# Second weight matrix of the first channel group converted inside the mixers' first run, with both stated orders written anew

## The chip, the cores and the metric

The kernel runs on one core of a Trainium2 chip. The metric is device time in microseconds (us). Three runs of the kernel before took 602.53, 602.62 and 603.88 us, so its median is 602.62 us. A further execution was profiled: it took 602.69 us, and its trace spans 600.90 us from the first instruction to the last. The other 1.79 us lie around the span.

## The reference

Attention with rotary positions for 4 batches of 8 heads (576 positions, 64 values a head), then a token mixer and a channel mixer, each two matrix products with a ReLU between them and a residual sum. Everything is float32 at the outside; the four weight matrices arrive as 64-bit floats.

```python
q_rot, k_rot = rotate(q), rotate(k)                       # 4 x 8 x 576 x 64
scores = q_rot @ k_rot.T / sqrt(64)
attn = softmax(scores)                                     # exp(scores - max) / (sum + 1e-9)
x = (attn @ v).transpose(0, 2, 1, 3).reshape(4, 576, 512)

h = relu(x.transpose(0, 2, 1) @ w_tok1) @ w_tok2           # 576 -> 256 -> 576
u = x + h.transpose(0, 2, 1)
out = u + relu(u @ w_ch1) @ w_ch2                          # 512 -> 1536 -> 512
```

## The kernel before, in words

Attention works on 16 pairs of heads. For each, the rotated q and k are transposed on TensorE, scores come in blocks (line L593), VectorE takes the row maxima (L493) and ScalarE the exponentials (L497), TensorE turns the result over (L616), ScalarE or VectorE copies it out of PSUM (L621), and TensorE multiplies with v (L634). VectorE scales by the row sums and writes X (L668; XT, L674, for the tail rows).

The mixers multiply in split form: each float32 operand is kept as a high and a low part, and three matmuls (high·high, low·high, high·low) stand for one product. The token mixer is L819 (first product) and L841 (second); its residual sum into X is L844. The channel mixer cuts the 576 x 4 rows into five chunks and the 1536 columns into four groups. For each chunk `up` transposes u (L910), casts the high part out of PSUM on ScalarE (`uh`, L915) and takes the low part on VectorE (`ul`, L916). `cm1` multiplies with the group's part of w_ch1 (L936: 36 matmuls for a chunk, then gh on ScalarE, L938, and gl on VectorE, L940). `cm2` multiplies with its part of w_ch2 (L963: 9 matmuls for each block of 128 rows, then the sum into X on VectorE, L965).

Weights go through `f64_split`, a chain of ten tasks for each block of 128 rows after its load (L738): ScalarE L709 (into fa) and L711 (into fc), a clamp L713 (VectorE or GpSimd), VectorE L715 (shift), L717 (into fh) and L719, a product L721 and a sum L723 (VectorE or GpSimd), the cast of the high part on ScalarE (L729) and the difference that gives the low part (L730, VectorE or GpSimd). There are two stg, two fa and two fh buffers and one fc. For a group, w_ch1 is four blocks of 128x384 (results c1h, c1l) and w_ch2 three blocks of 128x512 (c2h, c2l). Three blocks of eleven tasks are the 33 tasks of the title.

The order is set by a planner. `plan.run(ORDER1)` places 1666 tasks in a stated order, a number each that also picks the engine: attention, the token weights and the tokens of batch 0. `plan.run(ORDER2)` places 162 more, the mixers' first run: tokens of batches 1 to 3, w_ch1 of group 0, and `up` for chunks 0 and 1. A third call, `plan.run()` without an order, places the rest greedily, by when a task can start and by priority: `up` for chunks 2 to 4, all `cm1` and `cm2`, the weights of groups 1 to 3 and, in the kernel before, w_ch2 of group 0. Each engine then executes its own instructions in the order in which they were placed, and waits on the others by semaphores. PSUM has eight banks for the mixers (`m_...`).

```python
held = weights(0, AT["wg"][0], (1,))            # w_ch1 of group 0
for ci in range(2):
    ups[ci] = up(ci, AT["up"][ci])
plan.run(ORDER2)
...
weights(0, 1000, (2,), held)                     # w_ch2 of group 0
for ci in range(2, NC):
    ups[ci] = up(ci, 1000 + 100 * ci - 120)
```

Of the kernel before, what the change touches and what calls it, by code (L numbers as in the profile page):

```python
# [64 lines left out]

class Task:
# [8 lines left out]
class Plan:  # L75
# [53 lines left out]
    def place(self, t, s, eng, dur, fn):  # L129
# [13 lines left out]
        fn()  # L143
# [3 lines left out]
        self.clock[eng] = end  # L147
# [64 lines left out]
AT = {'load': [1.46, -95.74, 1755.84, -446.16, -10.32, -39.47], 'rot': [-30.33, -28.71, -413.29, -24.98], 'pt': [2461.71, -120.88, 1877.09, 0.03], 'qk': [-19.92, -94.77, -29.81, -42.47, -64.18, 1974.42, -445.69, 27.95, -11.96, -66.6, -413.71, -4.28, -3.14, 1684.05, 2036.62, 1632.15, 1700.12, -3.39, -14.08, 1717.83], 'mx': [-18.32, -97.08, -28.47, -222.21, 6.35, 102.54, -32.49, -15.54, 1579.98, 1593.71, -66.46, 1669.44, -16.89, 1934.18, 1942.38, -85.25, -54.68, -66.81, 1912.69, -8.83, 1697.35, 2415.63, 1609.9, 23.08, -40.85, -271.23, 8.19, -10.94, -20.04, -405.36, -59.72, -406.05, 2099.98, 1.92, 1651.83, 1951.2, 1677.89, 1499.17, -7.34, 1632.2], 'ex': [-19.75, -25.79, -97.92, -19.73, 1983.61, 1573.24, -17.98, -1.23, -9.94, -101.57, 88.51, 1713.87, -29.01, 1630.6, -9.17, 1879.5, 1922.03, -18.78, -23.18, 19.55], 'tr': [-261.73, 1684.38, -347.64, 1853.57, -223.18, 1740.33, -18.09, 1625.16, -353.85, 2050.66, -65.51, 2482.09, -74.23, -25.76, 1924.68, -6.29, -550.16, 2116.11, -49.33, -19.36], 'cp': [-285.8, 1993.92, -15.28, -338.61, -33.12, -32.9, 1494.57, -414.57, -230.35, -354.01, -214.2, -9.85, -35.68, -247.66, -14.87, -307.76, -26.24, 90.92, 1865.89, 2189.31], 'pv': [1983.73, 10.91, -453.58, -23.11], 'p1': [-52.7, -56.83, 1864.91, -1.75], 'fin': [2216.99, -20.0], 'tok': [1652.21, 1875.86, 1482.41, 2166.22, -11.87, 1947.96], 'inv': [-8.92, -3.44], 'f6': [1767.81, 1652.44], 'tk': [1968.59, -7.94, -26.45, -12.06], 'pre': [-2.55], 'tm': [-283.71, 77.1, 1499.3, -17.97, 1601.75, -59.36, 1543.29, -96.53, -111.26, 1974.16, 1626.79, -49.74], 'wg': [1621.69], 'up': [3.65, 1617.77], 'ti': [5.61]}  # L212
ORDER1 = (
# [106 lines left out]
def rope_attention_mixer_kernel(ctx: ExitStack, tc: tile.TileContext, q, k, v, w_tok1, w_tok2, w_ch1, w_ch2, tab, out):  # L320
# [8 lines left out]
    nc = tc.nc  # L329
# [28 lines left out]
    def attention(ctx):  # L358
# [703 lines left out]
```

## Time and profile before

| | us |
|---|---|
| median of three runs | 602.62 |
| profiled execution | 602.69 |
| its span | 600.90 |
| TensorE (PE) busy | 585.6 (97% of the span) |
| VectorE (DVE) busy | 385.3 (64%) |
| ScalarE (ACT) busy | 312.4 (52%) |
| GpSimd (POOL) busy | 309.3 (51%) |

Busy shares are averages over stages with different limits. Attention and the tokens of batch 0 fill the span up to about 251 us, the mixers' first run goes on to about 288 us for the first products and to 295 us for the last second product, and the channel mixer takes the rest. PE counts a matmul as busy up to a modelled end, so a stretch with 100% can still hold matmuls that follow one another a little late. PEld is the weight load that runs ahead of the matmuls.

### The profile page before, as it was taken

Reading aid. Unit: us, or ns where it says so; the run is one execution under the profiler, and the core shown is the slowest. Engines: PE = TensorE matmul, PEld = TensorE weight load, DVE = VectorE, ACT = ScalarE, POOL = GpSimd, SP = SyncE. Lnnn points to the kernel's source line nnn. Section 1 sums busy time; section 2 is a strip of 40 time slices with the busy share of each in tenths; the row PEclk is TensorE's granted clock in tenths of the full one; section 3 lists DMA queues with packets and bytes.
Section 4 is the critical chain, followed back from the end, with each engine's and each line's share of the span. In section 5 each row is a group of like instructions: output and inputs, shape, how many; then the busy total and the mean of one; then the engine's idle time right before and its main releaser. Section 6 shows DMA issues by size and latency. Waiting matters only on the chain.

```text
span 600.9 us, 12684 instructions
## 1 busy us (share of the span) xinstructions
PE 585.6 (97%) x4825; PEld 461.0 (77%) x4825; DVE 385.3 (64%) x1121; ACT 312.4 (52%) x796; POOL 309.3 (51%) x258
## 2 busy tenths in 40 slices
PE   4999999999999999999999999999999999999997
PEld 3777676777677777687777888888888888888886
DVE  6998999998899988688845545445423443223232
ACT  3998999999999988243464332233202311110110
POOL 4997876888868531023578686477503760000000
PEclk9999999999999999999998999999999999999999
DMA  5443242313311201001122222122101200001123
GB/s 151 126 116 86 71 108 75 105 29 90 101 52 60 62 2 31 25 26 62 36 65 76 71 61 54 60 71 55 50 1 36 71 0 1 1 1 70 71 70 106
DMA packets 34093, 36.15 MB, mean 60 GB/s; under 512 B 13808, under 2 KB 27632, under 8 KB 34032
## 3 DMA queue, kind: packets, MB, share of 16 engines
q1 hardware_dynamic: 33200, 35.01, 20.3%
q8 instruction: 38, 0.62, 0.4%
q10 hardware_dynamic: 832, 0.33, 0.2%
q14 instruction: 23, 0.19, 0.1%
HBM read 30.61 MB, written 4.72 MB: 59 GB/s over the span
## 4 chain that ended last, share of the span: by engine, by line
PE 95%; DVE 2%; DMA 1%; ACT 1%; issue 0%; DVEq 0%
PE m L936 25%; PE m L963 24%; PE s L634 14%; PE s L593 11%; PE s L616 7%; PE m L841 3%; PE m L819 3%; PE s L471 2%; PE s L516 2%; PE s L819 1%; PE s L537 1%; PE s L663 1%; PE s L841 1%; DMA tabs<-in_tab_dram 1%; DVE p L493 0%; DMA kraw<-in_k_dram 0%
## 5 line engine op out<-in xcount | busy, mean ns | idle before, releaser
L938 ACT ACTIVATE gh<-m 128x512 fp32r<-128x512 f32 (+1 forms) x60 | 33.3, 555 | 174.0 <-PE m L936 170.8
L497 ACT ACTIVATE p<-p,nm 128x576 f32<-128x576 f32 x128 | 98.9, 778 | 1.7 <-DVE p L493 1.1
L940 DVE SCALAR_TENSOR_TENSOR gl<-m,gh 128x512 fp32r<-128x512 f32 (+1 forms) x60 | 38.1, 637 | 93.3 <-ACT gh L938 93.2
L965 DVE TENSOR_TENSOR X<-m,X 128x512 f32<-128x512 f32 (+1 forms) x65 | 44.4, 683 | 74.0 <-PE m L963 73.9
L936 PE MATMUL m<-uh,c1h 128*128 128x512 f32 (+1 forms) x240 | 89.1, 371 | 0.1
L936 PE MATMUL m<-ul,c1h 128*128 128x512 f32 (+1 forms) x240 | 88.9, 370 | 0.0
L936 PE MATMUL m<-uh,c1l 128*128 128x512 f32 (+1 forms) x240 | 88.9, 370 | 0.0
L634 PE MATMUL s<-pt,vraw 128*64 128x256 f32 (+1 forms) x640 | 84.7, 411 | 0.0
L963 PE MATMUL m<-c2l,gh 128*128 128x512 f32 (+1 forms) x219 | 84.6, 386 | 0.0
L963 PE MATMUL m<-c2h,gh 128*128 128x512 f32 (+1 forms) x219 | 84.6, 386 | 0.0
L963 PE MATMUL m<-c2h,gl 128*128 128x512 f32 (+1 forms) x219 | 84.6, 386 | 0.0
L593 PE MATMUL s<-kt,qt 64*128 64x288 f32 x512 | 80.9, 430 | 1.2 <-ACT kt L482 0.9
L721 POOL TENSOR_TENSOR fa<-fc,fa 128x512 f32<-128x512 f32 (+2 forms) x30 | 35.9, 1197 | 75.2 <-DVE fa L719 63.4
L634 PEld LDWEIGHTS s<-pt,vraw 128*64 128x64 f32 x640 | 43.1, 137 | 30.1 <-DVE p L493 1.3
L493 DVE TENSOR_SCALAR_CACHE_REDUCE p<-s,nm 128x288 f32<-128x288 f32 x128 | 62.3, 512 | 3.8 <-PE s L593 1.7
L621 ACT COPY pt<-s 128x320 f32<-128x320 f32 (+1 forms) x172 | 60.6, 408 | 4.9 <-PE s L616 3.4
L616 PEld LDWEIGHTS s<-ident,p 64*128 64x128 f32 x1152 | 47.0, 139 | 17.5 <-ACT p L497 8.1
L593 PEld LDWEIGHTS s<-kt,qt 64*128 64x128 f32 x512 | 51.1, 192 | 8.7 <-ACT pt L621 1.7
L493 DVE TENSOR_SCALAR_CACHE_REDUCE p<-s 128x288 f32<-128x288 f32 x128 | 53.9, 452 | 4.4 <-PE s L593 4.0
L713 POOL TENSOR_SCALAR fa<-fa 128x512 f32<-128x512 f32 (+3 forms) x30 | 50.9, 1699 | 9.5 <-ACT fa L709 9.4
L616 PE MATMUL s<-ident,p 64*128 64x64 f32 x1152 | 52.6, 226 | 0.3 <-ACT p L497 0.2
L936 PEld LDWEIGHTS m<-uh,c1h 128*128 128x128 f32 x240 | 45.5, 190 | 8.1 <-DVE ul L916 0.3
(130 smaller groups left out, 1061.8 us busy)
## 6 DMA issues: line engine op xcount, KB each, us to landing
stg<-in_moe_w_ch_dram SPq DMA_DIRECT2D x16, 384.0 KB, 3.2
stg<-in_moe_w_ch_dram SPq DMA_DIRECT2D x12, 512.0 KB, 3.7
vraw<-in_v_dram SPq DMA_DIRECT2D x16, 256.0 KB, 3.2
kraw<-in_k_dram SPq DMA_DIRECT2D x15, 256.0 KB, 3.2
qraw<-in_q_dram SPq DMA_DIRECT2D x15, 256.0 KB, 3.3
out_dram<-X SPq DMA_DIRECT2D x15, 256.0 KB, 2.3
stg<-in_moe_w_tok_dram SPq DMA_DIRECT2D x4, 512.0 KB, 4.3
kraw<-in_k_dram SPq DMA_DIRECT2D x32, 32.0 KB, 2.9
```

Of the source, the lines that this page charges most:

```text
L493: return lambda: nc.vector.tensor_scalar(out=p()[:, c * W2:(c + 1) * W2], in0=sb.t[:, 0:W2], scalar1=-D ** -0.5, scalar2=nm.t[:, 0:1] if c ...
L497: return lambda: nc.scalar.activation(out=p(), in_=p(), func=ACTF.Exp, bias=nm.t[:, 1:2], scale=-1.0, accum_out=l())
L593: nc.tensor.matmul(sbs[h].t[:, 0:W2], flat(qt.t)[halves[h], TL + j * P:TL + (j + 1) * P], flat(kt.t)[halves[h], TL * (1 - h) + u * W2:TL * ...
L616: nc.tensor.transpose(xy[z].t[:, i * TL:(i + 1) * TL], pb.t[halves[z], c0:c0 + P], ident[halves[z], halves[z]])
L621: return lambda: e(out=pt[c].t[:, R * h:R * h + m, o + z * TL:o + (z + 1) * TL], in_=xy[z].t[:, 0:m * TL].rearrange("p (r s) -> p r s", r=m))
L634: nc.tensor.matmul(ab.t[halves[h], 0:w], vb.t[:, h, r, :], m, start=(r == 0), stop=(r == R))
L713: clamp = lambda e: lambda: e.tensor_scalar(out=A(), in0=A(), scalar1=EXP_LO, scalar2=EXP_HI, op0=ALU.max, op1=ALU.min)
L721: mul_ = lambda e: lambda: e.tensor_tensor(out=A(), in0=C(), in1=A(), op=ALU.mult)
L936: nc.tensor.matmul(tb.t[:, 0:n], a, m, start=(i == 0), stop=(i == len(lst) - 1))
L940: y = add("DVE", dve(n), lambda f=f, tb=tb: nc.vector.scalar_tensor_tensor(out=gb.t[1][:, f, 0:n], in0=tb.t[:, 0:n], scalar=0.0, in1=gb.t[ ...
L963: nc.tensor.matmul(tb.t[:, 0:w], a, m, start=(i == 0), stop=(i == len(lst) - 1))
L965: y = add("DVE", dve(w) + 0.08, lambda u=u, tb=tb, cols=cols, w=w: nc.vector.tensor_tensor(out=u[:, cols], in0=tb.t[:, 0:w], in1=u[:, cols ...
```

## The change

The call that makes the 33 conversion tasks of w_ch2, group 0, now stands ahead of `plan.run(ORDER2)`. ORDER2 has 195 entries in place of 162, and all of them are new. ORDER1 has the same 1666 tasks and is written anew as well; 166 of them run on another engine than before (the copies L621 for one: 160 on ScalarE where there were 172). The third, greedy run has the same priorities as before, without these 33 tasks.

The diff also brings code for pairs of PSUM banks that are read by one instruction (`duo`, `Half`, `none`, `mx1`, `cp1`, `f51` and a few more). It acts only on numbers listed in `MERGED`, which is empty. `clock` may no longer go back in the planner, and the buffers of a task are listed once each.

```diff
+MERGED = ()
 ORDER1 = (
-    68, 84, 0, 16, 88, 8, 20, 24, 28, 36, 4, 92, 12, 96, 104, 40, 44, 48, 76, 100, 52, 64, 72, 60, 80, 108, 112, 116, 148, 156, 152, 32, 56, 1408, 1428,
+    68, 0, 84, 16, 20, 88, 24, 92, 96, 100, 28, 12, 4, 8, 40, 32, 44, 104, 48, 52, 64, 60, 56, 72, 80, 76, 36, 1464, 108, 112, 116, 120, 132, 128, 1472,
...
 ORDER2 = (
-    6688, 6692, 7056, 7060, 6680, 6700, 6696, 6684, 7252, 6665, 7064, 6668, 7232, 7256, 6708, 6673, 6676, 6704, 7068, 6716, 7072, 7076, 7080, 6784, 6788,
+    7056, 7064, 6692, 6688, 6696, 7100, 7104, 7113, 7060, 7116, 6700, 6680, 7120, 7124, 7068, 7232, 7252, 6664, 6668, 6704, 6708, 7072, 7076, 6672, 7244,
...
+        def duo():
+            duos[0] += 1
+            if duos[0] - 1 in MERGED:
+                b = Buf(banks, True)
+                return b, [Half(b, 0), Half(b, 1)]
+            return None, [Buf(banks), Buf(banks)]
...
-        self.clock[eng] = end
+        self.clock[eng] = max(self.clock[eng], end)
...
         for ci in range(2):
             ups[ci] = up(ci, AT["up"][ci])
+        weights(0, AT["wg"][0] + 1000, (2,), held)
         plan.run(ORDER2)
...
         held[0].users -= 1
-        weights(0, 1000, (2,), held)
         for ci in range(2, NC):
             ups[ci] = up(ci, 1000 + 100 * ci - 120)
```

The diff shifts the lines: L668 becomes L724, L709 to L730 become L773 to L794, L844 becomes L908, L910 becomes L974, L916 becomes L980, L936 becomes L1000, L940 becomes L1004, L963 becomes L1027 and L965 becomes L1029.

The first place is VectorE at the end of attention, its last rows before the mixers' first run. X_59 and XT_63 take the second token product of batch 0 there, X_62 the last outputs of attention. In the kernel before:

```order
L668 TENSOR_TENSOR X_62<-s,ri_132 128x4x64
L844 TENSOR_TENSOR XT_63<-s,XT_63 64x512
L668 TENSOR_TENSOR X_62<-s,ri_131 128x4x64
L844 TENSOR_TENSOR X_59<-s,X_59 128x512 x2
L668 TENSOR_TENSOR X_62<-s,ri_132 128x4x64
```

In the changed kernel:

```order
L908 TENSOR_TENSOR X_59<-s,X_59 128x512
L730 TENSOR_TENSOR XT_64<-s,rt_136 64x64
L724 TENSOR_TENSOR X_62<-s,ri_132 128x4x64
L908 TENSOR_TENSOR X_59<-s,X_59 128x512 x2
L908 TENSOR_TENSOR XT_63<-s,XT_63 64x512
```

The last output of attention (X_62) stood behind the token sums and now stands ahead of them.

The second place is GpSimd (POOL) around the end of the mixers' first run; c1l and c2l are the low parts of the two matrices of group 0. In the kernel before:

```order
L730 TENSOR_TENSOR c1l_3986<-fh_70,c1h_3985 128x384
L730 TENSOR_TENSOR c1l_3986<-fh_69,c1h_3985 128x384
L713 TENSOR_SCALAR fa_68<-fa_68 128x512
L713 TENSOR_SCALAR fa_67<-fa_67 128x512
L721 TENSOR_TENSOR fa_68<-fc,fa_68 128x512
L723 TENSOR_TENSOR fh_70<-fh_70,fa_68 128x512
L721 TENSOR_TENSOR fa_67<-fc,fa_67 128x512
L730 TENSOR_TENSOR c2l_3988<-fh_70,c2h_3987 128x512
```

In the changed kernel:

```order
L857 TENSOR_TENSOR xs_88<-X_62,xs_88 128x512
L787 TENSOR_TENSOR fh_70<-fh_70,fa_67 128x512
L794 TENSOR_TENSOR c1l_3986<-fh_69,c1h_3985 128x384
L794 TENSOR_TENSOR c2l_3988<-fh_70,c2h_3987 128x512
L785 TENSOR_TENSOR fa_68<-fc,fa_68 128x512
L785 TENSOR_TENSOR fa_67<-fc,fa_67 128x512
L787 TENSOR_TENSOR fh_70<-fh_70,fa_67 128x512
L794 TENSOR_TENSOR c2l_3988<-fh_69,c2h_3987 128x512
```

The first block of w_ch2 is now through the chain before the last token work on this engine is done (xs is the split of X for the token mixer), and the clamps of its blocks stand on VectorE.

The third place is VectorE where `up` of chunks 2 to 4 takes its low parts (ul) out of the PSUM banks. In the kernel before these follow on `cm1` of chunk 1:

```order
L940 SCALAR_TENSOR_TENSOR gl_4361<-m_3978,gh_4360 128x512
L715 TENSOR_SCALAR fa_68<-fa_68 128x512
L940 SCALAR_TENSOR_TENSOR gl_4361<-m_3981,gh_4360 128x512
L916 TENSOR_TENSOR ul_3994<-m_3984,uh_3993 128x8x64
L717 SCALAR_TENSOR_TENSOR fh_70<-stg_66,fa_68 128x512
L916 TENSOR_TENSOR ul_3994<-m_3983,uh_3993 128x8x64
L719 TENSOR_SCALAR fa_68<-fh_70 128x512
L916 TENSOR_TENSOR ul_3994<-m_3980,uh_3993 128x8x64
L916 TENSOR_TENSOR ul_3994<-m_3982,uh_3993 128x8x64
L916 TENSOR_TENSOR ul_3996<-m_3979,uh_3995 128x8x64
```

In the changed kernel the greedy run has placed `cm2` of chunks 0 and 1 ahead of them (X_59 and X_60 take its results):

```order
L1029 TENSOR_TENSOR X_60<-m_3981,X_60 128x512
L779 TENSOR_SCALAR fa_68<-fa_68 128x512
L1029 TENSOR_TENSOR X_60<-m_3982,X_60 128x512
L1029 TENSOR_TENSOR X_60<-m_3984,X_60 128x512
L781 SCALAR_TENSOR_TENSOR fh_69<-stg_65,fa_68 128x512
L980 TENSOR_TENSOR ul_3994<-m_3979,uh_3993 128x8x64
L980 TENSOR_TENSOR ul_3994<-m_3980,uh_3993 128x8x64
L980 TENSOR_TENSOR ul_3994<-m_3978,uh_3993 128x8x64
L980 TENSOR_TENSOR ul_3994<-m_3983,uh_3993 128x8x64
L980 TENSOR_TENSOR ul_3996<-m_3977,uh_3995 128x8x64
```

The two conversion steps that stood between the first three ul have moved: one ahead of them, the other (L719, now L783) behind the eighth. On TensorE the 80 transposes of these three `up` stood behind `cm1` of chunk 1 and ahead of all `cm2`; now they stand behind `cm2` of chunk 1 and ahead of `cm1` of chunk 2.

## Rows read from the trace of the kernel before

**Rows 1.** The page's chain that ended last: shares of the span by engine.

```profile
PE 95%; DVE 2%; DMA 1%; ACT 1%; issue 0%; DVEq 0%
```

**Rows 2.** By stretch: length, busy us of PE, PEld, DVE, ACT, POOL; then PEclk.

```profile
30.00:250.00 220.00, 219.67 (x2878) 159.14 (x2876) 196.47 (x753) 200.60 (x567) 150.99 (x122) 1.00 0.25 69
252.80:288.30 35.50, 35.50 (x209) 28.47 (x209) 29.67 (x53) 12.83 (x24) 8.76 (x7) 1.00 0.12 38
...
295.30:311.50 16.20, 16.20 (x73) 13.20 (x71) 7.97 (x13) 6.37 (x11) 13.06 (x10) 1.00 0.18 57
311.50:317.00 5.50, 3.66 (x81) 3.01 (x80) 4.69 (x9) 5.27 (x12) 2.50 (x3) 1.00 0.29 74
317.70:321.10 3.40, 3.40 (x10) 2.63 (x9) 2.90 (x7) 1.26 (x3) 2.67 (x3) 0.50 0.00 0
321.10:590.00 268.90, 268.90 (x1255) 225.54 (x1255) 108.28 (x184) 61.68 (x114) 104.42 (x83) 1.00 0.15 46
```

**Rows 3.** The page's groups, attention's weight loads: busy, mean | idle before, releaser.

```profile
L634 PEld LDWEIGHTS s<-pt,vraw 128*64 128x64 f32 x640 | 43.1, 137 | 30.1 <-DVE p L493 1.3
...
L616 PEld LDWEIGHTS s<-ident,p 64*128 64x128 f32 x1152 | 47.0, 139 | 17.5 <-ACT p L497 8.1
L593 PEld LDWEIGHTS s<-kt,qt 64*128 64x128 f32 x512 | 51.1, 192 | 8.7 <-ACT pt L621 1.7
```

**Rows 4.** Chain of waits, 246 to 345 us: start, duration, engine, line.

```profile
251.12 1.19 DVE X L844 x2
252.32 0.34 DVE X L668
...
252.80 2.98 PE m L819 x12
...
295.33 16.33 PE m L936 x72
...
315.17 1.80 DVE ul L916 x3
...
317.02 7.35 PE m L936 x24
324.37 8.16 PE m L963 x36
332.53 2.72 PE m L936 x12
```

**Rows 5.** Timeline around the ups of chunks 2 to 4: start, duration, engine.

```profile
311.58 0.28 PE L910 MATMUL m<-ident,XT 64*128 64x64 f32 x2
...
312.33 4.57 ACT L915 CAST uh<-m 128x512 fp32r<-128x512 f32 x10
...
313.56 0.68 DVE L717 SCALAR_TENSOR_TENSOR fh<-stg,fa 128x512 uint32<-128x512 uint32 x1
...
314.89 0.27 PE L910 MATMUL m<-ident,XT 64*128 64x64 f32 x1 [0.93 <-DVE ul L916]
...
318.30 0.63 PE L936 MATMUL m<-ul,c1h 128*128 128x512 f32 x1
```

**Rows 6.** Timeline of DVE behind a cm2 unit.

```profile
332.57 0.69 DVE L965 TENSOR_TENSOR X<-m,X 128x512 f32<-128x512 f32 x1 [1.35 <-PE m L963]
```

**Rows 7.** DVE by line, 252.66 to 288.3: busy, mean | idle before, releaser.

```profile
L827 DVE SCALAR_TENSOR_TENSOR rs<-m,rs 128x512 fp32r<-128x512 f32 x6 | 3.9, 683 | 1.1 <-ACT rs L824 1.1
...
L791 DVE CAST xs<-X 128x512 fp32r<-128x512 f32 x6 | 2.6, 425 | 1.8 <-PE m L819 1.7
...
L713 DVE TENSOR_SCALAR fa<-fa 128x384 f32<-128x384 f32 x3 | 1.1, 354 | 1.8 <-ACT fa L709 1.8
```

**Rows 8.** Timeline of DVE, two shifts (L715) in the mixers' first run.

```profile
271.94 0.36 DVE L715 TENSOR_SCALAR fa<-fa 128x384 uint32<-128x384 uint32 x1
...
278.84 1.33 DVE L715 TENSOR_SCALAR fa<-fa 128x384 uint32<-128x384 uint32 x1
```

**Rows 9.** Timeline of POOL beside the second of these.

```profile
278.50 1.46 POOL L793 TENSOR_TENSOR xs<-X,xs 128x512 fp32r<-128x512 f32 x1
```

More of the change, by code (lines that the diff above doesn't have):

```diff
@@ L63, in t, with __init__ @@
         return self.held[2]
+class Half:
+    def __init__(self, buf, z):
+        self.buf = buf
+        self.z = z
+    @property
+    def t(self):
+        return self.buf.t[:, self.z]
 class Task:
@@ L91, in add @@
         t.deps = [d for d in deps if d is not None]
-        t.bufs = list(bufs)
+        t.bufs = list(dict.fromkeys(getattr(b, "buf", b) for b in bufs))
         for b in t.bufs:
@@ L142, in place @@
                 b.slots.taken += 1
-        fn()
+        if fn:
+            fn()
+        else:
+            end = -1e9
         t.end, t.eng = end, eng
@@ L395, in attention, with none @@
         ready, ready_v, couple = {}, {}, {}
+        duos = [0]
+        def duo():
[4 more added lines that the diff above has]
+            return None, [Buf(banks), Buf(banks)]
+        def none(deps, bufs):
+            return add("DVE", 0.0, None, deps, bufs)
         order_tr = [None]
@@ L461, in prep @@
                                  for z0, z1 in ((0, R + 1),)]
-                    xy = [Buf(banks), Buf(banks)]
+                    one, xy = duo() if n else (None, [Buf(banks), Buf(banks)])
                     split = r0 > 0
@@ L475, in prep, with cq1 @@
                     t = add("PE", 0.06 * (r1 - r0) + 0.012, tr, x, [*xy, ub, tb], pp, mode="row")
-                    for z in range(2):
+                    if one:
+                        def cq1(e, one=one, tb=tb, m=R + 1):
+                            return lambda: e(out=tb.t.rearrange("p (r z) s -> p z r s", z=2)[:, ::-1],
+                                             in_=one.t[:, :, 0:m * TL].rearrange("p z (r s) -> p z r s", s=TL))
+                        done += [none([t], [one, tb]), both(cq1, 2 * (R + 1) * TL, [t], [one, tb], pp)]
+                    for z in range(0 if one else 2):
                         m = r1 - r0 - (z and split)
@@ L494, in mx, with mx1, score_banks @@
                                                    scalar2=nm.t[:, 0:1] if c else None, op0=ALU.mult, op1=ALU.min, accum_out=nm.t[:, c:c + 1])
+        def mx1(sb, nm, p):
+            return lambda: nc.vector.tensor_scalar(out=p(), in0=sb.t.rearrange("p a s -> p (a s)")[:, 512 - W2:512 + W2], scalar1=-D ** -0.5,
+                                                   scalar2=None, op0=ALU.mult, op1=ALU.min, accum_out=nm.t[:, 1:2])
+        def score_banks():
+            d = [duo() for _ in range(2)]
+            return [[h[1][u] for h in d] for u in range(2)], [h[0] for h in d]
         def ex(nm, p, l):
@@ L509, in tails @@
             t = []
+            sb2, ones = score_banks()
             for u in range(2):
-                sbs = [Buf(banks), Buf(banks)]
+                sbs = sb2[u]
                 def qk(sbs=sbs, u=u):
@@ L515, in qk @@
                         for h in range(2):
-                            nc.tensor.matmul(sbs[h].t[halves[x ^ h], 0:W2], flat(qt[x].t)[halves[h], 2 * R * TL + TL:2 * R * TL + 2 * TL],
+                            c0 = 512 - W2 if ones[h] and not u else 0
+                            nc.tensor.matmul(sbs[h].t[halves[x ^ h], c0:c0 + W2], flat(qt[x].t)[halves[h], 2 * R * TL + TL:2 * R * TL + 2 * TL],
                                              flat(kt[x].t)[halves[h], TL + u * W2:TL + (u + 1) * W2], start=True, stop=True)
@@ L523, in tails @@
                 x = None
-                for u in range(2):
+                if ones[h]:
+                    none([t[0][0]], [ones[h], nms_[h], pbs[h]])
+                    x = add("DVE", 0.68, mx1(ones[h], nms_[h], p), [t[1][0]], [ones[h], nms_[h], pbs[h]])
+                for u in range(0 if ones[h] else 2):
                     x = add("DVE", 0.44 if u else 0.38, mx(t[u][1][h], nms_[h], p, u), [t[u][0], x], [t[u][1][h], nms_[h], pbs[h]],
@@ L587, in pair, with qk @@
                 t = []
+                sb2, ones = score_banks()
                 for u in range(2):
-                    sbs = [Buf(banks), Buf(banks)]
-                    def qk(sbs=sbs, j=j, u=u):
+                    sbs = sb2[u]
+                    def qk(sbs=sbs, j=j, u=u, ones=ones):
                         for h in range(2):
-                            nc.tensor.matmul(sbs[h].t[:, 0:W2], flat(qt.t)[halves[h], TL + j * P:TL + (j + 1) * P],
+                            c0 = 512 - W2 if ones[h] and not u else 0
+                            nc.tensor.matmul(sbs[h].t[:, c0:c0 + W2], flat(qt.t)[halves[h], TL + j * P:TL + (j + 1) * P],
                                              flat(kt.t)[halves[h], TL * (1 - h) + u * W2:TL * (1 - h) + (u + 1) * W2], start=True, stop=True)
@@ L600, in pair @@
                     x = None
-                    for u in range(2):
+                    if ones[h]:
+                        none([t[0][0]], [ones[h], nmb[h], pb])
+                        x = add("DVE", 0.68, mx1(ones[h], nmb[h], p), [t[1][0]], [ones[h], nmb[h], pb])
+                    for u in range(0 if ones[h] else 2):
                         x = add("DVE", 0.44 if u else 0.38, mx(t[u][1][h], nmb[h], p, u), [t[u][0], x], [t[u][1][h], nmb[h], pb], g + AT["mx"][20 * odd + 4 * i + 2 * u + h])
@@ L608, in pair @@
                 for h in range(2):
-                    xy = [Buf(banks), Buf(banks)]
+                    one, xy = duo()
                     m = R + h
@@ L618, in pair, with cp1 @@
                     x = order_tr[0] = add("PE", 0.06 * m + 0.006, tr, [*xs[0:h + 1], order_tr[0]], [*xy, pb, pt[c]], at("tr", h), mode="row")
-                    for z in range(2):
+                    if one:
+                        def cp1(e, one=one, c=c, o=o, h=h, m=m):
+                            return lambda: e(out=pt[c].t[:, R * h:R * h + m, o:o + P].rearrange("p r (z s) -> p z r s", z=2),
+                                             in_=one.t[:, :, 0:m * TL].rearrange("p z (r s) -> p z r s", r=m))
+                        ev[c] += [none([x], [one, pt[c]]), both(cp1, 2 * m * TL, [x], [one, pt[c]], 0.0)]
+                    for z in range(0 if one else 2):
                         def cp(e, z=z, xy=xy, c=c, o=o, h=h, m=m):
@@ L653, in pair @@
             tinv, rt = tail_inv[n]
-            xy = [Buf(banks), Buf(banks)]
+            one, xy = duo()
             cs = hp * 2 * D
@@ L675, in f6, with f51 @@
                                             in1=rt.t[0:TL, c:c + 1].to_broadcast([TL, D]), op=ALU.mult)
-                x_done.setdefault(b, []).append(add("DVE", dve(R * D), f5, [x, inv], [xy[z], rb], pf))
+                def f51():
+                    nc.vector.tensor_tensor(out=X[b][:, :, cs:cs + 2 * D].rearrange("p r (z d) -> p z r d", z=2),
+                                            in0=one.t[:, :, 0:R * D].rearrange("p z (r d) -> p z r d", r=R),
+                                            in1=rb.t[:, 0:R].rearrange("p r z -> p z r").unsqueeze(3).to_broadcast([P, 2, R, D]), op=ALU.mult)
+                if one and not z:
+                    x_done.setdefault(b, []).append(none([x, inv], [one, rb]))
+                else:
+                    x_done.setdefault(b, []).append(add("DVE", dve(2 * R * D) if one else dve(R * D), f51 if one else f5, [x, inv], [xy[z], rb], pf))
                 def f6a(z=z, c=c):
```

143 rows, old and new, of tables (ORDER1, ORDER2) are left out of this document.

## The prediction

> **What bounds the kernel now.** I read the chain of waits by engine first: TensorE (PE) holds 95% of it, VectorE 2%, ScalarE and DMA 1% each [rows 1]. So a gain must come from a place where PE stands still or runs slowly. Next the stretches [rows 2]: PE is busy for 219.67 of 220 us in attention, for all of the mixers' first run up to 288.3 us, for all of 295.3 to 311.5 us and for all of 321.1 to 590 us. Two places are left. Between 311.5 and 317.0 us it is busy for 3.66 of 5.50 us, and right behind that, from 317.7 to 321.1 us, the granted clock is 0.50, the lower of its two levels (1.2 in place of 2.4 GHz), after a stretch of transposes and waits. The chain of waits and the timeline then say who is late there [rows 4, 5], and the same chain shows a smaller hole at 251 to 253 us, where PE waits for the last sums of VectorE.
>
> **The change part by part.**
>
> *The hole at 311.6 us.* Before, the transposes of three `up` follow on `cm1` of chunk 1. They begin at 311.58 us [rows 5] and `cm1` of chunk 2 begins at 317.02 us [rows 4]: 5.44 us. These `up` fill twelve banks and eight exist, so the last transposes and then the first bank of `cm1` wait for five ul in turn; the first such wait is at 314.89 us, released by ul [rows 5]. Two conversion steps stand among these ul: L717, 0.68 us at 313.56 [rows 5], and L719 behind it. Three ul in a row take 1.80 us, 0.60 each [rows 4]. In the changed kernel both steps are gone from between the ul. What comes late instead is the sum of the last `cm2` block and one L781 (the old L717) ahead of the first ul. A sum starts 0.04 us after PE has gone on to other work (PE at 332.53 [rows 4], sum at 332.57 [rows 6]). With T as the start of the transposes: sum at T + 0.04, L781 0.60 later, first ul at T + 1.24. Before, the uh casts began 0.75 us after the transposes (312.33 [rows 5]) and the first ul needs one of 0.6 us, the pitch of such operations, so T + 1.35 is the later bound, and I take that. The fifth ul starts 4 x 0.60 later, lasts 0.68 and PE follows 0.04 behind: T + 4.5. Against 5.44 that is a gain of 0.9 us. Ends: the two steps wholly off the path, 1.3 us gained; uh or L781 a step late, nothing gained. The 80 transposes themselves cost the same at either place.
>
> *The clock behind it.* The 24 matmuls from 317.02 us took 7.35 us [rows 4]. Twelve took 2.72 us at full clock, so 24 would take 5.44 us: the low level cost 1.9 us. The waits on ul shrink by about half in the changed kernel, from 1.84 us without PE work (5.50 less 3.66) to some 0.9, and ahead of them stand 72 matmuls of `cm2` where 72 of `cm1` stood. At the end of attention the chain lies on VectorE from 251.12 us until PE goes on at 252.80, at most 1.7 us without PE work, and the clock of the stretch behind it is 1.00 [rows 2, 4]. So a wait of about that length does not bring the clock down here; I take the whole 1.9, with nothing as the other end.
>
> The Trainium skill, "TensorE: Matmul & The Clock Gate", section "Part 4: PE-mode transpose", says that transposes do not count as PE work for the gate in the way matmuls do. By that rule the clock would fall after the move as well, since the same 80 transposes stand there in one piece; the row with 0.50 behind them fits it, and it is my second case below.
>
> *End of attention.* VectorE's chain before is two sums of 1.19 us and then X_62, 0.34 us, before PE may go on [rows 4]. Now X_62 stands ahead of the sums, so PE waits for the sums alone: a gain of 0.3 us. If another sum is late it is nothing.
>
> *33 tasks in the first run.* They now stand beside the token mixer. Up to 288.3 us PE has 35.50 us of its own work and VectorE 29.67, ScalarE 12.83, GpSimd 8.76 [rows 2]. VectorE gets five instructions more (58 against 53 by the two programs' order), by the mean of 0.56 us (29.67 over 53) 2.8 us more: 32.5, still under PE's 35.5; the others have room by far. I cost this at nothing; PE's matmuls hide it. If that cover is gone, the price is in the slower case. The conversions that leave 295 to 311 us free VectorE and GpSimd where PE was 100% busy anyway: nothing. Moving `cm2` of chunks 0 and 1 ahead of the `up` changes no count of matmuls: nothing. Group 1's conversions move with it and run beside 16 us of `cm2` with little on VectorE.
>
> *The new order of attention.* By the two programs' order TensorE's sequence is nearly the same, and it changes its array mode 195 times in place of 197. What can move is waiting: the weight loads sat idle 1.3, 8.1 and 1.7 us behind p and pt [rows 3], 11.1 us in all, much of it while the matmul before still ran. So at most 11 us may be won. At most as much may be lost, if waits double. VectorE (196.47 of 220) and ScalarE (200.60) are nearly full there [rows 2], so order matters; nothing in the trace gives the sign. I take nothing. The inert code costs nothing: `MERGED` is empty.
>
> *Sum.* 0.9 + 1.9 + 0.3 = 3.1 us off the profiled 602.69: 599.6 us. The profiled run is 0.07 us above the median of the three, which changes nothing at this size. A measurement of this kernel tells about 0.3%, 1.8 us, from no change.
>
> **The rivals.**
>
> *The clock falls all the same.* For it: the transposes stay together and still wait. Against it: the wait is half as long, and a wait of up to 1.7 us did nothing at 251 us. Only 0.9 + 0.3 us is left: 601.5 us, within 0.3%.
>
> *Attention's new order wins as well.* For it: 8.1 us of waits on p alone [rows 3], and 166 tasks on other engines. Against it: PE is 99.8% busy there. A fifth of the 11.1 us, 2.2, gives 597.4 us.
>
> *Slower: VectorE bounds the mixers' first run.* It works 29.67 us there and stands idle for others: 1.1 for rs, 1.8 for PE, 1.8 for fa and little more [rows 7], 4.7 together. With 2.8 us more that is 37.2 against PE's 35.5: 1.7 us over. On top, the stretch gets four more clamps and shifts on VectorE, and a shift that met a GpSimd operation took 1.33 us where one alone took 0.36 [rows 8]; the operation beside it began at 278.50 and ran 1.46 us [rows 9]. Three of four such meetings cost 2.9 us more. 1.7 + 2.9 - 3.1 is 1.5 us slower, and with the idle time growing by the same steps (each new fa to wait for adds 0.6, 1.8 over 3) about 2.4: 605.0 us. It decides as soon as PE's waits in that run pass 3.1 us. Against it: idle time is partly slack that a new instruction fills, and PE did not wait once in 35.5 us.
>
> The Trainium skill, "SBUF — State Buffer", section "Who interferes with whom", says that VectorE in its two-port modes and GpSimd shut each other out for a whole instruction, whoever came first. The pair of rows at 278.5 us agrees: the shift ended as the GpSimd operation did. It speaks against bringing both engines' conversion work into this run.
>
> *Slower: attention's order loses.* With waits up by half of the 11.1 us, 5.5, the time is 599.6 + 5.5, so 605.1 us. The same rows as for the win speak for and against.
>
> *The conversion isn't done in time.* `cm2` of chunk 0 now follows `cm1` of chunk 1, at about 311.6 us, 12.8 us earlier than before (324.37 [rows 4]). If c2l is late by half of this, 6.4 us, the time is 606.0 us and the hole has only changed its name. Against it: the first of three blocks is through GpSimd ahead of the last token work.
>
> **How the numbers follow.** Forecast 0.45 at 599.6; clock falls 0.21 at 601.5; attention wins 0.14 at 597.4; VectorE bounds 0.09 at 605.0; attention loses 0.06 at 605.1; too late 0.05 at 606.0. The likeliest case alone spans 599.2 to 600.8 by the ends of the hole (0 to 1.3 us) and of attention's end (0 to 0.3). The range from 597.4 to 604.0 us leaves out half of the win, 0.07, and some two thirds of the three slow cases, 0.13, since their prices are ends rather than middles. Faster by over 0.3%: the forecast, the win and a little of the second case, 0.61; slower by as much: most of the last three, 0.17; the rest, 0.22, is no change.
>
> **What would show it.** Right: from the first transpose of `up` for chunk 2 to `cm1` of chunk 2 about 4.5 us, five ul behind one another at 0.60; granted clock 1.00 in the stretch behind; attention's end to the first L883 of the mixers 0.3 us shorter; PE 100% busy in the first run; attention as long as before, within 0.5 us. Wrong: a clock of 0.50 behind the `up` or anywhere new, PE waiting for rs, ul or X in the first run, `cm2` of chunk 0 waiting for c2l, or attention's end moved by over a microsecond. The last is the likeliest way for the forecast to miss, since the order of 1666 tasks is new and the trace can't price it.

## The result, and the profile after

The changed kernel takes 610.45 us (median of four runs, 610.29 to 611.91) against 602.58 us: a ratio of 1.0133, with a 95% interval from 1.011 to 1.0156. The forecast was 599.6 us; the kernel became slower by 7.9 us. Its profiled execution took 610.57 us with a span of 608.80.

Three marks on TensorE divide the 7.9 us: the first matmul of the mixers' first run, the first `cm1`, and the end. The first is in the timeline of TensorE in the changed kernel (columns: start, duration, engine, line; in brackets the idle time ahead and what ended it), together with the other waits of that run and the first transpose of the late `up`:

```profile
259.72 0.70 PE L883 MATMUL m<-xs,w1h 128*128 128x512 f32 x2 [0.87 <-DVE XT L908]
...
290.99 0.72 PE L905 MATMUL m<-rs,w2h 128*128 128x512 f32 x2 [1.03 <-DVE X L908]
...
295.65 0.50 PE L883 MATMUL m<-xt,w1th 128*128 128x512 f32 x1 [1.63 <-DVE xt L857]
...
338.31 0.28 PE L974 MATMUL m<-ident,XT 64*128 64x64 f32 x2
```

The second and the hole at the `up` are in its chain of waits (start, duration, engine, line):

```profile
305.74 16.32 PE m L1000 x72
322.06 16.33 PE m L1027 x72
...
339.02 0.68 DVE fh L781
339.71 3.06 DVE ul L980 x5
...
342.81 16.61 PE m L1000 x72
```

Before, the first run began at 252.80 us and `cm1` at 295.33 [rows 4]; now at 259.72 and 305.74. So attention takes 6.9 us longer, the first run 3.5 us longer (46.02 in place of 42.53), and the rest, up to the span's end, 2.5 us less (303.06 in place of 305.57). That sums to 7.9 us.

*The hole at the `up`* is as forecast. The transposes follow the 72 `cm2` matmuls, one L781 and five ul in a row follow, and `cm1` goes on at 342.81 us: from the first transpose at 338.31 that is 4.50 us in place of 5.44 [rows 4, 5]. The granted clock from there to the end of the kernel is 1.00. The 72 matmuls behind the hole took 16.61 us, 0.3 more than the 72 at 305.74, where 24 had lost 1.9 us before.

*The first run* is not hidden. TensorE waits for X at 290.99 us and for xt at 295.65, with VectorE busy nearly without a gap from 286.1 to 299 us. The two waits make 2.7 of the 3.5 us; the rest is a slower pace of the same 239 matmuls (busy 43.35 us in place of 42.53). VectorE's timeline shows why it is late there:

```profile
266.15 0.69 DVE L857 TENSOR_TENSOR xs<-X,xs 128x512 fp32r<-128x512 f32 x1 [1.18 <-ACT xs L855]
...
286.12 1.35 DVE L857 TENSOR_TENSOR xs<-X,xs 128x512 fp32r<-128x512 f32 x1 [0.35 <-ACT xs L855]
287.40 1.50 DVE L781 SCALAR_TENSOR_TENSOR fh<-stg,fa 128x512 uint32<-128x512 uint32 x1
288.93 1.40 DVE L783 TENSOR_SCALAR fa<-fh 128x512 uint32<-128x512 uint32 x1
...
294.19 1.41 DVE L857 TENSOR_TENSOR xt<-XT,xt 64x512 fp32r<-64x512 f32 x1
...
298.93 0.68 DVE L781 SCALAR_TENSOR_TENSOR fh<-stg,fa 128x512 uint32<-128x512 uint32 x1
...
299.86 0.42 DVE L783 TENSOR_SCALAR fa<-fh 128x512 uint32<-128x512 uint32 x1
```

and the timeline of GpSimd what ran beside these steps:

```profile
285.91 1.01 POOL L785 TENSOR_TENSOR fa<-fc,fa 128x384 f32<-128x384 f32 x1 [2.08 <-DVE fa L783]
287.00 1.34 POOL L787 TENSOR_TENSOR fh<-fh,fa 128x384 f32<-128x384 f32 x1
288.31 1.74 POOL L857 TENSOR_TENSOR xs<-X,xs 128x512 fp32r<-128x512 f32 x1
...
294.05 1.00 POOL L794 TENSOR_TENSOR c1l<-fh,c1h 128x384 fp32r<-128x384 f32 x1
```

The step L781 takes 0.68 us at 298.93 and 1.50 at 287.40, L783 0.42 at 299.86 and 1.40 at 288.93; the splits L857 take 1.35 and 1.41 where such a difference takes 0.69 at 266.15. Each long one overlaps a GpSimd operation and ends 0.3 to 0.6 us after that one. This is the shift of 1.33 us of the kernel before [rows 8, 9], which ended 0.2 us after the GpSimd operation beside it, met again and again. Over the whole first run, taking for each VectorE instruction what it lasted beyond the shortest tenth of its line and shape, and only where that is over 0.15 us, eight instructions lost 6.9 us, where two lost 1.8 us before. All ten overlap a GpSimd operation. The one that begins first keeps its length: L783 at 299.86 us begins 0.02 us ahead of a GpSimd operation of 1.55 us and takes its plain 0.42.

*Attention* stands still longest near 160 us, by the stretches (length, busy time of PE, PEld, DVE, ACT, POOL, then the granted clock):

```profile
150.00:160.00 10.00, 8.85 (x112) 6.37 (x106) 8.51 (x24) 8.35 (x25) 8.48 (x8) 1.00 0.52 152
160.00:165.00 5.00, 3.24 (x34) 1.91 (x34) 4.39 (x18) 2.32 (x6) 3.68 (x3) 0.67 0.01 3
```

TensorE is idle for 1.15 us in the first, nearly all of it near 151 us, and for 1.76 us in the second, whose clock is 0.67. The second wait and what VectorE did just before:

```profile
161.76 2.19 PE L559 MATMUL s<-kt,qt 64*64 64x288 f32 x14 [1.78 <-DVE p L526]
```

```profile
156.11 1.04 DVE L777 TENSOR_SCALAR fa<-fa 128x512 f32<-128x512 f32 x1
...
157.45 1.40 DVE L781 SCALAR_TENSOR_TENSOR fh<-stg,fa 128x256 uint32<-128x256 uint32 x1
158.88 1.91 DVE L857 TENSOR_TENSOR xt<-XT,xt 64x512 fp32r<-64x512 f32 x1
```

and what GpSimd did beside it:

```profile
155.32 1.56 POOL L465 TENSOR_TENSOR w<-qraw,tabs 128x640 f32<-128x640 f32 x1
156.82 1.74 POOL L467 TENSOR_TENSOR uq<-qraw,tabs 128x640 f32<-128x640 f32 x1
158.53 1.71 POOL L465 TENSOR_TENSOR w<-kraw,tabs 128x640 f32<-128x640 f32 x1
```

A clamp, an and-or on 256 columns and a split, 4.35 us together, stand ahead of the row maxima (L526) that TensorE waits for, and rotation products fill GpSimd at the same time, back to back.

### The profile page after: what moved, and what is told of

Read it like the earlier page. It is cut to its first block, busy times and chain, and to the rows that moved or that the text cites. A ratio compares the mean times of both kernels' runs of the same rounds, so it can differ in the third digit from the quotient of the medians.

```text
span 608.8 us, 12712 instructions
## 1 busy us (share of the span) xinstructions
PE 587.9 (97%) x4825; PEld 460.1 (76%) x4825; DVE 390.7 (64%) x1118; ACT 314.1 (52%) x797; POOL 309.4 (51%) x260
## 4 chain that ended last, share of the span: by engine, by line
PE 50%; DVE 3%; ACT 0%; POOL 0%; issue 0%; ACTq 0%
PE m L1000 24%; PE m L1027 24%; PE m L905 1%; DVE ul L980 1%; DVE fh L781 0%; DVE xs L857 0%; PE m L883 0%; DVE fa L779 0%; DVE fa L783 0%; DVE xt L857 0%; DVE XT L908 0%; DVE X L908 0%; PE m L974 0%; ACT xs L855 0%; POOL fa L785 0%
## 5 line engine op out<-in xcount | busy, mean ns | idle before, releaser
L1004 DVE SCALAR_TENSOR_TENSOR gl<-m,gh 128x512 fp32r<-128x512 f32 (+1 forms) x60 | 38.3, 638 | 98.0 <-ACT gh L1002 98.0
L1029 DVE TENSOR_TENSOR X<-m,X 128x512 f32<-128x512 f32 (+1 forms) x65 | 44.4, 683 | 68.9 <-PE m L1027 68.7
L1000 PE MATMUL m<-uh,c1h 128*128 128x512 f32 (+1 forms) x240 | 88.4, 368 | 0.1
L1000 PE MATMUL m<-ul,c1h 128*128 128x512 f32 (+1 forms) x240 | 88.3, 368 | 0.0
L1000 PE MATMUL m<-uh,c1l 128*128 128x512 f32 (+1 forms) x240 | 88.3, 368 | 0.0
L1027 PE MATMUL m<-c2l,gh 128*128 128x512 f32 (+1 forms) x219 | 84.6, 386 | 0.0
L1027 PE MATMUL m<-c2h,gh 128*128 128x512 f32 (+1 forms) x219 | 84.6, 386 | 0.0
L1027 PE MATMUL m<-c2h,gl 128*128 128x512 f32 (+1 forms) x219 | 84.5, 386 | 0.0
L785 POOL TENSOR_TENSOR fa<-fc,fa 128x512 f32<-128x512 f32 (+3 forms) x32 | 37.6, 1175 | 68.8 <-DVE fa L783 66.3
L526 DVE TENSOR_SCALAR_CACHE_REDUCE p<-s,nm 128x288 f32<-128x288 f32 x128 | 61.9, 512 | 3.7 <-PE s L641 2.1
L667 PEld LDWEIGHTS s<-ident,p 64*128 64x128 f32 x1152 | 45.7, 140 | 19.3 <-ACT p L538 5.6
L677 ACT COPY pt<-s 128x320 f32<-128x320 f32 (+1 forms) x160 | 55.6, 407 | 5.9 <-PE s L667 4.9
L526 DVE TENSOR_SCALAR_CACHE_REDUCE p<-s 128x288 f32<-128x288 f32 x128 | 54.0, 452 | 6.4 <-PE s L641 5.1
L777 POOL TENSOR_SCALAR fa<-fa 128x384 f32<-128x384 f32 (+3 forms) x27 | 45.1, 1674 | 15.5 <-ACT fa L773 15.5
L1000 PEld LDWEIGHTS m<-uh,c1h 128*128 128x128 f32 x240 | 45.2, 189 | 8.0 <-DVE ul L980 0.3
```

The costliest lines, as they stand in the source:

```text
L526: return lambda: nc.vector.tensor_scalar(out=p()[:, c * W2:(c + 1) * W2], in0=sb.t[:, 0:W2], scalar1=-D ** -0.5, scalar2=nm.t[:, 0:1] if c ...
L667: nc.tensor.transpose(xy[z].t[:, i * TL:(i + 1) * TL], pb.t[halves[z], c0:c0 + P], ident[halves[z], halves[z]])
L677: return lambda: e(out=pt[c].t[:, R * h:R * h + m, o + z * TL:o + (z + 1) * TL], in_=xy[z].t[:, 0:m * TL].rearrange("p (r s) -> p r s", r=m))
L777: clamp = lambda e: lambda: e.tensor_scalar(out=A(), in0=A(), scalar1=EXP_LO, scalar2=EXP_HI, op0=ALU.max, op1=ALU.min)
L785: mul_ = lambda e: lambda: e.tensor_tensor(out=A(), in0=C(), in1=A(), op=ALU.mult)
L1000: nc.tensor.matmul(tb.t[:, 0:n], a, m, start=(i == 0), stop=(i == len(lst) - 1))
```

## The experiments

The theory I took from this is that one mechanism makes both losses: a VectorE step that reads two SBUF tiles, or a clamp or shift, that meets a running GpSimd operation has to wait for its end, so where the new orders bring the two together VectorE becomes late and TensorE waits. The rival for the first run is that VectorE simply has more instructions there; the rival for attention that the three steps stand in a bad place, whatever they last.

**One part at a time.** The first two kernels swap only the table ORDER1:

```diff
# e1: the changed kernel
-ORDER1 = (68, 0, 84, 16, 20, ...)      # as changed
+ORDER1 = (68, 84, 0, 16, 88, ...)      # as before
# e2: the kernel before
-ORDER1 = (68, 84, 0, 16, 88, ...)
+ORDER1 = (68, 0, 84, 16, 20, ...)
```

> The changed kernel with the kernel before's stated order of attention (ORDER1); the new ORDER2 and the early conversion of w_ch2 stay. If the three parts add up as the trace of the changed kernel reads (attention about 6.5 us longer, the mixers' first run about 3.7 us longer, the hole at the ups about 2.7 us shorter), attention's 6.5 us go and the time is 602.6 + 3.7 - 2.7 = 603.6 us. Rival: the first run is late only because the new attention order leaves VectorE and GpSimd behind at its end; then its 3.7 us go too and the time is about 599.9 us.

Measured: 603.85 us, ratio to the kernel before 1.0034 (1.0021 to 1.0047). `cm1` starts 3.7 us later than before (295.33 [rows 4]), as in the chain of waits of e1, and the steps in its first run last as long as in the changed kernel:

```profile
279.50 1.33 DVE xs L857
280.82 1.43 DVE fh L781
...
282.28 1.40 DVE fa L783
...
287.53 1.43 DVE xt L857
...
299.07 16.32 PE m L1000 x72
```

So the first run's loss comes from the new ORDER2 and the early conversion alone, and doesn't need the new attention order.

> The kernel before with the new ORDER1 alone; ORDER2 and the place of the conversion as before. If the order of attention costs by itself what the trace shows, 602.6 + 6.5 = 609.1 us, with a stretch near 160 us where TensorE waits for VectorE and the clock is low for a while. Rival: the new ORDER1 fits only the new ORDER2 and the loss shifts; then the time is well off 609.1, below 606 or above 611 us.

Measured: 608.1 us, ratio 1.010 (1.0085 to 1.0115), a loss of 6.0 us against the 602.15 us of the kernel before in that session. The parts nearly add up: 1.7 (e1) and 6.0 (e2) against 7.9.

**Is it the meeting with GpSimd?** In e4, made from e1, GpSimd's clamps, products, sums and splits of X in the first run work on 16 columns, so part of the conversion and of the split is left out; its low parts c1l and c2l stay whole, and so do GpSimd's count of instructions, all orders and VectorE's work.

```diff
+        part = lambda e, v: v[:, 0:16] if thin[0] and e is nc.gpsimd else v
-        mul_ = lambda e: lambda: e.tensor_tensor(out=A(), in0=C(), in1=A(), op=ALU.mult)
+        mul_ = lambda e: lambda: e.tensor_tensor(out=part(e, A()), in0=part(e, C()), in1=part(e, A()), op=ALU.mult)
...
+        thin[0] = True
         plan.run(ORDER2)
+        thin[0] = False
```

> The kernel of e1 (old ORDER1, new ORDER2), and in the mixers' first run GpSimd's clamps, products, sums and its differences for xs work on 16 columns only, so that part of the conversion and of the token mixer's low parts is left out; every instruction stays on its engine and in its place, and VectorE's work is unchanged. If VectorE is late in the first run because its conversion steps are shut out while GpSimd's operations run (nine of its steps took 9.5 us longer than their usual time in the changed kernel, three took 3.9 us longer in the kernel before), the waits of TensorE there go nearly wholly: e1 less 3.5 us, about 600.1 us. Rival: VectorE is late because it has more instructions; then the time stays within 1 us of e1.

Measured: 600.2 us, ratio 0.9976 (0.9965 to 0.9987): the 3.65 us are gone, as the theory said, and `cm1` starts as early as before the change:

```profile
295.24 16.32 PE m L1003 x72
```

Three long steps are left in its first run, beside the c1l and c2l of GpSimd, and TensorE doesn't wait for them. The expectation says nine steps with 9.5 us and three with 3.9; the traces have eight with 6.9 us in the changed kernel and two with 1.8 before, which changes nothing in what it tests.

The control puts the same edit into the kernel before:

> The kernel before with the same 16-column GpSimd operations in the mixers' first run as e4 (part of the conversion and of the low parts left out). Control for e4: TensorE does not wait in the first run of the kernel before, so the theory says nothing is gained there, 602.2 us, within 1 us. Rival: shorter GpSimd operations speed the kernel up in some other way, and e4's 3.65 us are that: about 598.5 us.

Measured: 601.53 us against 602.45, ratio 0.9987 (0.9975 to 1.0). That is 0.9 us, at most 1.5 by the interval, so 2 us or more of e4's 3.65 need the crowded first run. Even the 0.9 us are the clock's (more on it below): six of ten runs of e7 have a mean granted clock of 0.999, against three of 19 of the kernel before in that session, and both sets take 601.29 us in the mean. At equal clock the edit gains nothing here, and 3.8 us between e1 and e4 (603.87 and 600.09 us in the mean of the runs with 1.00). Thin GpSimd operations also shorten GpSimd's own part in a conversion; e4 can't tell this from the shutting out. The chain of e1 above speaks for the shutting out: four steps of 1.33, 1.43, 1.40 and 1.43 us stand in it whose usual times are 0.68, 0.68, 0.42 and 0.68, 3.1 us together.

**The operations by themselves.** In the kernel m1 VectorE does six operations of a kind, first alone and then while GpSimd multiplies.

```python
for one in kinds:              # shift; and-or; difference of two SBUF tiles; sum with PSUM
    for _ in range(6): one()
    ...
    for i in range(8):
        nc.gpsimd.tensor_tensor(out=(g1, g2)[i % 2], in0=g0, in1=z, op=ALU.mult)
    for _ in range(6): one()
```

> A kernel of nothing but the disputed operations; it computes none of the reference. Six VectorE operations of one kind on 128x512, alone, and then the same six while GpSimd runs eight products of 128x512 (1.3 us each) that read and write SBUF: the shift (L715's kind), the and-or of L717, a difference of two SBUF tiles, and a sum with one operand in PSUM. If VectorE is shut out for a whole GpSimd operation, the shift goes from about 0.42 us to 1.3 to 1.8 us each and the sum with a PSUM operand stays at 0.68. For the kinds with two SBUF operands the theory says the same as for the shift (0.68 to some 1.3 to 2). Rival: both engines share the port in turns and everything on VectorE becomes 1.2 to 1.6 times as long, the shift 0.5 to 0.7.

In the timeline of VectorE of m1 (the second row of each line is the one beside GpSimd):

```profile
6.21 2.72 DVE L40 TENSOR_SCALAR fa<-fa 128x512 uint32<-128x512 uint32 x6
...
10.02 8.33 DVE L40 TENSOR_SCALAR fa<-fa 128x512 uint32<-128x512 uint32 x6
...
21.12 4.31 DVE L41 SCALAR_TENSOR_TENSOR fb<-sg,fa 128x512 uint32<-128x512 uint32 x6
...
26.18 9.94 DVE L41 SCALAR_TENSOR_TENSOR fb<-sg,fa 128x512 uint32<-128x512 uint32 x6
...
38.89 4.32 DVE L42 TENSOR_TENSOR fd<-fa,fb 128x512 f32<-128x512 f32 x6
...
44.35 9.94 DVE L42 TENSOR_TENSOR fd<-fa,fb 128x512 f32<-128x512 f32 x6
...
57.05 4.31 DVE L43 TENSOR_TENSOR fd<-m,fd 128x512 f32<-128x512 f32 x6
...
62.39 4.31 DVE L43 TENSOR_TENSOR fd<-m,fd 128x512 f32<-128x512 f32 x6
```

and of GpSimd, its eight products beside each:

```profile
9.81 10.88 POOL L52 TENSOR_TENSOR g<-g,z 128x512 f32<-128x512 f32 x8
...
25.97 12.49 POOL L52 TENSOR_TENSOR g<-g,z 128x512 f32<-128x512 f32 x8
...
62.30 9.81 POOL L52 TENSOR_TENSOR g<-g,z 128x512 f32<-128x512 f32 x8
```

Six shifts go from 2.72 to 8.33 us, six and-ors and six differences from 4.3 to 9.94, and the sums with one operand in PSUM stay at 4.31. GpSimd pays less: its eight products take 9.81 us beside the sums, 10.88 beside the shifts, 12.49 beside the others. The rates fit whole instructions in turn: 9.94 over 6 is 1.66 us, one product (1.23) and some 0.4 us of VectorE's step of 0.72, the part that doesn't overlap it (an estimate from these rows). The rival with 1.2 to 1.6 times the length is out. The Trainium skill, "SBUF — State Buffer", section "Who interferes with whom", says that VectorE instructions with two SBUF inputs, and those in a two-port mode, which `tensor_scalar` can enter, contend with GpSimd, and that one with at most one SBUF input outside these modes doesn't. The four pairs of rows agree; the numbers are theirs.

**Attention.** In e5, made from e2, four rotation operations of GpSimd do one of their five parts, so most of this rotation is left out.

```diff
+THIN = (("q", 13, 0), ("q", 13, 1), ("q", 13, 2), ("k", 12, 0))
...
+                        r1 = r0 + 1 if (nm, n, i) in THIN else end
```

> The kernel of e2 (new ORDER1 alone), in which four GpSimd operations of the rotation (the three of q of pair 13 and the first of k of pair 12) work on one of five parts of their columns, so that most of this rotation is left out; order and VectorE's work are unchanged. These four run from 154.8 to 161.7 us of the trace of e2, beside a clamp of 1.04, an and-or of 1.39 and a split of 1.91 us on VectorE, which take 0.42, 0.42 and 0.68 us elsewhere. If VectorE was shut out, TensorE's wait of 1.77 us and the low clock behind it go, and with them about 3.5 us: 604.6 us. Rival: the new order puts these three steps ahead of the row maxima and their plain length is enough for the stall; then the time stays within 1 us of e2's 608.1.

Measured: 604.83 us in the median of ten runs (603.35 to 606.41), 3.3 us below e2 and 2.4 above the kernel before (ratio 1.0038, 1.0026 to 1.005). The three steps have their plain length in the timeline of VectorE (L715 and L795 are the clamp and the split here, L719 the and-or):

```profile
155.44 0.42 DVE L715 TENSOR_SCALAR fa<-fa 128x512 f32<-128x512 f32 x1
...
156.15 0.42 DVE L719 SCALAR_TENSOR_TENSOR fh<-stg,fa 128x256 uint32<-128x256 uint32 x1
156.60 0.68 DVE L795 TENSOR_TENSOR xt<-XT,xt 64x512 fp32r<-64x512 f32 x1
```

and TensorE neither waits nor slows down behind them, by the stretches of e5 and then of e2:

```profile
159.00:162.00 3.00, 3.00 (x54) 2.06 (x47) 2.63 (x13) 3.00 (x11) 0.52 (x1) 1.00 0.02 5
162.00:166.00 4.00, 4.00 (x72) 2.94 (x68) 3.18 (x14) 3.95 (x13) 1.49 (x2) 1.00 0.02 4
```

```profile
159.00:162.00 3.00, 1.23 (x13) 0.50 (x14) 2.99 (x9) 0.68 (x1) 3.00 (x3) 1.00 0.00 0
162.00:166.00 4.00, 4.00 (x40) 3.27 (x34) 2.62 (x13) 3.83 (x12) 1.21 (x1) 0.59 0.01 4
```

So in e2's trace three long steps, 2.8 us too long, made a hole of 1.8 us and a stretch at clock 0.59, and over half of the loss of the new order goes with them. Runs of like mean clock (0.996 and 0.997) say the same: 608.1 us in e2, 605.1 in e5 and 602.45 in the kernel before, so 3.0 of 5.6 us. No run puts this edit into the kernel before, so a part that comes from GpSimd's shorter operations themselves isn't excluded. The other 2.4 us are mostly waits at other places: in e5 TensorE stands idle 1.6 us longer than before between 30 and 250 us (218.11 us busy against 219.67 [rows 2]), 1.1 of it near 150 us, and 1.2 us longer between 10 and 30 us (18.37 busy against 19.58), but some 0.8 us shorter at the two ends of attention. What causes these waits no run shows.

**The hole and the clock.** In e3, the changed kernel, the `up` are chained ahead of `cm2` of chunks 0 and 1 again:

```diff
-                t = add("PE", ..., tr, [u_done[z] for u in us for z in u[2]], tb, pr, mode="row")
+                t = add("PE", ..., tr, [u_done[z] for u in us for z in u[2]] + [order[0]] * chain, tb, pr, mode="row")
+                order[0] = t if chain else order[0]
...
+                        for cj in range(2, NC):
+                            ups[cj] = up(cj, 1000 + 100 * cj - 120, chain=True)
+                        for cj, gd, gb, pr in early:
+                            cm2(cj, g, gd + [order[0]], cb, wd, gb, pr + 150)
```

> The changed kernel with both new orders, but the three late ups chained ahead of cm2 of chunks 0 and 1, where they stood before. If the place of the ups is what shortened the hole (5.44 to 4.42 us) and kept the clock up behind it (1.9 to 0.3 us lost), both come back: 610.45 + 2.6 = 613.1 us. Rival: the hole is as short as now because conversion steps are no longer due among the ul, wherever the ups stand, and the clock falls or not by chance; then 610.5 to 611.5 us.

Measured: 609.84 us (608.73 to 610.48), no slower than the changed kernel. My theory of the place fell. In its chain five ul follow one another as in the changed kernel, and the clock holds behind them:

```profile
323.35 3.00 DVE ul L981 x5
...
326.40 8.45 PE m L1028 x36
```

Where the `up` stand doesn't matter. What is left to have shortened the hole is that no conversion steps are due among the ul any more, since w_ch2 was done before; no run tests this by itself.

And the same hole doesn't always bring the same clock. By the chain of waits it is 4.42 us long in the changed kernel (338.39 to 342.81), in e1 (331.72 to 336.14) and in e4 (327.89 to 332.31), with the same instructions; the stretches behind it, of e1 and then of e4:

```profile
338.00:343.00 5.00, 5.00 (x24) 4.14 (x23) 4.50 (x10) 2.94 (x5) 3.89 (x3) 1.00 0.12 17
```

```profile
327.00:332.00 5.00, 4.22 (x84) 3.35 (x82) 4.08 (x7) 3.44 (x8) 0.32 (x1) 1.00 0.32 101
332.00:338.00 6.00, 5.86 (x23) 4.58 (x20) 4.46 (x11) 2.73 (x8) 2.66 (x2) 0.72 0.02 6
```

Clock 1.00 in one and 0.72 in the other; the 72 matmuls behind the hole take 16.61 us in e1 and 18.27 in e4. Of the 12 runs of e4, eight (599.95 to 600.32 us) have a mean clock of 1.00 and four (601.4 to 602.1) of 0.996 or 0.997. The kernel before does the same: of its 36 runs in these sessions, ten at 600.9 to 601.6 us have 0.999, the others, 602.08 us and up, 0.997 or less. Only the profiled runs show where the clock fell, and no run shows what decides it.

**A faster version.** In v1 the kernel before keeps both of its orders, and the three `up` are chained one by one behind `cm1` of chunks 0, 1 and 2:

```diff
-        for ci in range(2, NC):
-            ups[ci] = up(ci, 1000 + 100 * ci - 120)
...
                 gd = cm1(ci, ups[ci], cb, wd, gb, pr)
+                if not g and ci + 2 < NC:
+                    ups[ci + 2] = up(ci + 2, pr + 80, chain=True)
                 cm2(ci, g, gd, cb, wd, gb, pr + 150)
```

> The kernel before, with both of its stated orders, but the three late ups are chained between the cm1 of the chunks: up 2 behind cm1 0, up 3 behind cm1 1, up 4 behind cm1 2. Nothing is moved into the first run. If the hole of 5.44 us was made of 80 transposes in one block that outrun the eight banks, 80 transposes at 1.15 us for 32 take 2.9 us and 2.5 us of waits go; the low clock behind it (1.9 us) goes too: 602.6 - 4.4 = 198.2 + 400 = 598.2 us. Rival: the low clock comes from the transposes themselves, wherever they stand, and only the waits go: 600.1 us. Second rival: cm2 of chunk 0 then waits for w_ch2, and little is gained: 601 to 603 us.

Measured: 598.97 us (598.66 to 599.52), ratio 0.9952 (0.994 to 0.9965), faster than both kernels. Its chain has no hole left:

```profile
295.69 8.16 PE m L937 x36
303.85 1.15 PE m L910 x32
```

A whole `up` costs its transposes, 1.15 us for 32, and the matmuls of `cm1` run on at 305.00 us; the mean clock is 0.999 or 1.00 in all five runs. Against the ten runs of the kernel before with 0.999 (601.24 us in the mean) it gains 2.3 us, near the 2.5 us of waits in the expectation; the rest is the clock. It gains what the change was to gain, without moving one conversion.

## Why the prediction was wrong

*What bounds the kernel* was read rightly: TensorE, with one hole of 5.44 us.

*The hole*: 0.9 us forecast, 0.9 measured (5.44 to 4.50), by the row of ul that was forecast. That the moved `up` had a part in it, as the clock's argument put it, was wrong (e3).

*The clock*: 1.9 us taken whole. In the trace it came so, but partly by luck: both e4 and the kernel before show that the same hole lowers the clock in some runs and not in others; between the two kinds of run lie 1.2 us in the kernel before (601.24 and 602.45 in the mean) and 1.6 in e4. The mean clock was low in 26 of 36 runs of the kernel before and in five of the 17 of e1 and e4, so the term was worth some 0.5 to 0.7 us on average (an estimate from these shares). The rival in which the clock falls all the same came true in some runs. The argument that a wait of about 1.7 us does not bring the clock down fell too: behind 1.78 us in attention it was 0.50. In the changed kernel's profiled run the clock falls at the stall in attention instead, so its mean is 0.997 all the same.

*The end of attention*: 0.3 us, of no weight, and right: TensorE waited 0.87 us there, for XT, where it had waited 1.27 us for X_62. This gain lies within the 6.9 us.

*"33 tasks in the first run ... I cost this at nothing; PE's matmuls hide it"* is the step that failed first. The sum of busy times (32.5 of 35.5 us) was taken as cover. The sum itself even came out, by luck: VectorE is busy 32.58 us in the first 35.5 us of the run, but with 52 instructions and not 58. The cover left out that the added steps meet GpSimd's operations, and then each lasts two to four times as long. Over the whole run VectorE is busy 42.93 us in place of 36.08 (70 instructions, 64 before), and 5.1 of these 6.9 us are longer durations. The row that says so, 1.33 us against 0.36, was in my hands [rows 8, 9], and I used it for a rival of 0.09. Measured: 3.5 us.

*"The new order of attention ... I take nothing"* failed too, by 6.9 us in the trace and 6.0 in e2. More than half of the 6.0 goes with the same shutting out, in a stretch where VectorE works 196 of 220 us [rows 2] (e5). The rest is waits at other places, whose cause is open.

*The rivals.* "VectorE bounds the mixers' first run" named the place and the mechanism; its loss, 3.5 us, lies between its 1.7 and its 1.7 + 2.9. "Attention's order loses" was priced at 5.5 us. Each came true near its price, and both at once, with the hole's gain beside them: 602.7 - 2.5 + 3.5 + 6.9 is 610.6 us. I had set them up as cases that exclude each other, so no case and no end of the range held their sum. "Conversion too late" did not happen: `cm2` follows `cm1` without a wait in the chain at 322.06 us.

## What to carry to other kernels

Cover is not a sum of busy times: before work is moved beside other work, look in the trace for instructions of that kind whose duration varies, see what ran beside the long ones, and price each new meeting at the long duration. A whole new order of a full stretch deserves a slow case as likely as the fast one, and cases on different stretches add up. If a block of short work outruns its buffers, spread it between long matmul blocks; here that was worth more than moving the work that got in its way.

## What the runs showed of the hardware

Two things I had not expected in this size. A shift of 128x512 on VectorE goes from 0.45 to 1.39 us (2.72 and 8.33 over six) as long as GpSimd is multiplying in SBUF, while a sum with one operand in PSUM doesn't notice it at all (4.31 us for six either way). And one and the same hole of 4.4 us on TensorE, 80 transposes with 0.9 us of waits among them, left the granted clock at its upper level in e1's trace and took it to the lower one, 0.50, in e4's; between e4's runs with a mean clock of 1.00 and those with 0.997 or less lie 1.6 us. In the changed kernel's trace a wait of 1.78 us in attention brought it down as well, but two of e3's four runs, with the same order of attention, have a mean of 1.00.
